# A float32 FNet/SwiGLU mix on one core: the first transform block takes a product of raw data ahead of one of sums, and second forms are made as one row of three results

## The chip, the core and the metric

The kernel runs on one core of one Trainium2 chip. The metric is the device time of one execution in microseconds (us); the median of three runs of the kernel before is 682.49 us.

## The reference, cut to what matters

```
g = sigmoid((x * gate_w).sum(-1))            # x: 2048 x 512, all float32
a = x @ dft_hid_re.T ; b = x @ dft_hid_im.T
y = dft_seq_re @ a - dft_seq_im @ b          # A: the Fourier mixing
h = silu(x @ w1) * (x @ w3)                  # B: w1, w3: 512 x 1376
z = h @ w2                                   # w2: 1376 x 512
out = g * y + (1 - g) * z
```

## The kernel before, in words

**Precision.** TensorE multiplies float32 data rounded to a shorter form (fp32r). Each operand is therefore kept as two parts: the *high* part is the rounded value, made by ScalarE (`high`, L110), and the *low* part is the operand minus its high part, made by VectorE (`low`, L113). `mm3` (L126) makes one product from three matmuls, high x high, high x low and low x high, all issued at L124. In the profile, `zo<-B` on ACT is a high part and `zo<-B,zo` on DVE is a low part.

**Fewer products.** Each matrix product is made in 2 x 2 blocks by the Strassen-Winograd scheme, with seven block products in place of eight. So each operand has forms: four raw blocks (`B11`, `B12`, `B21`, `B22`) and four sums of them (`T1` to `T4`) on the moving side, and seven such forms on the stationary side. VectorE makes the sums (L669 for T1, T2 and T4, L672 for T3).

**Stages.** (1) The gate stage, to about 207 us, makes h for 22 items (11 chunks of w1 and w3, two halves of x). `gate_up(n)` works through item n. Into its lists `early`, `mid` and `at_end` the program puts spare work, such as the forms of w2: for item n of `W2_AT`, `sums_w2` runs in `early` of n, `high_w2` in `mid` of n and `low_w2` in `early` of n+1. (2) The transform stage: blocks 0 to 3 (kind F) multiply the sequence matrices by x, blocks 4 and 5 (H) multiply h by w2, blocks 6 and 7 (Y) apply the hidden matrices.

**The order inside a transform block.** `CHAIN` (L614) lists the seven products with the form of the moving operand that each takes: P1 B11, P5 T1, P6 T2, P3 B22, P7 T3, P2 B21, P4 T4. An F block has 4 steps for each, 28 in all, numbered m; one step is 12 matmuls. Step m needs a tile `zo` with the high and low part of its operand. `advance(m)`, called after the matmuls of step m are issued, loads raw data up to eight steps ahead, makes the sum for step m+4 and splits the operand for step m+3. There are four `zo` tiles, so the high part for step m+4 can be written only when TensorE has finished step m. All engines run their instructions in the order in which the program issues them (`manual_schedule`, L398).

**Stationary forms of x.** Block products P1, P5, P6 and P3 take the forms A1 (made in the gate stage); P7, P2 and P4 take the forms A2, which block 0 itself makes, for eight row groups p = 0 to 7, out of reloaded x (`xs`). `third_a2(p)` makes a 256-wide difference on VectorE (`sum2`, L174), then its high and its low part; `first_a2(p)` splits two raw 256-wide blocks as one 512-wide row. `A2_AT` gives the steps at which load, third and first are issued.

**Results.** When the last step of a product is done, its PSUM banks are read out: P5, P6 and P7 by ScalarE (`read`, L922), and P2, P3, P7 and P4 are finished on VectorE by adds and products with the gate (L929, L954, `spill` L815) and stored. P1, P6, P7 and P4 accumulate in the same pair of banks, P5 and P3 in a second pair, P2 in a third. In block 0, P3's result is put off to step 24 (L947); the other results follow their product at once.

**The start.** Before the loop over items, forms of x (`xo`) are made by hand-placed instructions (L477 to L504); the low part of T1 is put into `early` of item 1 (L510).

Of the kernel before, what the change touches and what calls it, by code (L numbers as in the profile page):

```python
# [21 lines left out]
NG = NST // 2  # L22
# [4 lines left out]
K = 9  # L27
W2_AT = (9, 11, 13, 15)
A1_AT = (12, 14, 16, 17, 18, 19, 20)
A2_AT = ((4, 8, 8), (5, 9, 9), (6, 10, 10), (7, 11, 11),  # L30
         (8, 13, 17), (9, 14, 18), (10, 15, 18), (11, 16, 19))


@with_exitstack
def fnet_swiglu_gate_kernel(
# [20 lines left out]
    nc = tc.nc  # L56
# [52 lines left out]
    def high(hi, src):  # L109
        nc.scalar.activation(hi, src, AF.Copy)  # L110

    def low(hi, lo, src):
        nc.vector.tensor_sub(lo, src, hi.bitcast(F32))  # L113

    def split(hi, lo, src):
        high(hi, src)
        low(hi, lo, src)
# [25 lines left out]
    def flat(ap):  # L143
        return ap.rearrange("p a n -> p (a n)")
# [28 lines left out]

    def sum2(r):  # L174

        nc.vector.tensor_sub(r[:, :256], r[:, 256:512], r[:, :256])  # L176
# [28 lines left out]
    def sum_xo(g, k, t):  # L205
        ST[g, k] = t
        nc.vector.tensor_sub(t, *(ST[g, v] for v in SUMS[k]))  # L207
# [80 lines left out]
    def first2(n):  # L288
        prod(G[n][1], n, 1, 1, False, True)
# [36 lines left out]
    early, ahead, second, mid, at_end = {}, {}, {}, {}, {}  # L326
# [167 lines left out]
    x3 = prod1(3)  # L494
    gate1(1)
    sum_xo(0, "T3", ST[0, "B12"])
    first2(2)
    seed(3, x3)
    high(*xo_parts(0, "T3")[::2])
# [6 lines left out]
    def do(work, n, f, *a):  # L506
        work.setdefault(n, []).append(lambda: f(*a))


    do(early, 1, lambda: low(*xo_parts(0, "T1")))  # L510
    do(ahead, 1, lambda: split_xo(0, "T4"))
    do(second, 1, free, *(ST[0, b] for b in ("B11", "B21", "B12", "B22")))
    do(early, 1, gate1, 2)
# [20 lines left out]
    def w2_parts(p):  # L534
        r, m, t1, t2 = W2R[p]
        return [*((flat(t1[:, 0, i:j]), flat(t1[:, 1, i:j]), v) for i, j, v in
                  ((0, 1, r[:, 256:512]), (1, 4, m[:, :768]))),
                *((flat(t2[:, 0, i:j]), flat(t2[:, 1, i:j]), v) for i, j, v in
                  ((0, 2, r[:, 512:]), (2, 3, r[:, :256])))]

    def sums_w2(p):
        W2R[p] += [wide(f"w2m{p}"), parts(f"w2a{p}"), parts(f"w2b{p}")]
        r, m, t1, t2 = W2R[p]
        sums1(r, m)
        nc.vector.tensor_sub(r[:, :256], r[:, 256:512], r[:, :256])

    def high_w2(p):
        for v in w2_parts(p):
            high(*v[::2])

    def low_w2(p):
        a, b, c, d = w2_parts(p)
        low(*a)
        low(*b)
        nc.gpsimd.dma_start(w2sp[0][p], W2R[p][2].bitcast(F32))
        low(*c)
        low(*d)
        nc.gpsimd.dma_start(w2sp[1][p], W2R[p][3][:, :, :3].bitcast(F32))
        free(*W2R.pop(p))

# [55 lines left out]

    NB = NTB + 4
    KIND = "F" * NTB + "HHYY"
    ORDER = [CHAIN] * (NB - 1) + [tuple(CHAIN[i] for i in (0, 5, 1, 2, 3, 4, 6))]
    NQ = [{"F": NG // 2, "H": NP2 // 2, "Y": KD // 2}[k] for k in KIND]  # L620
    STEPS = [(blk, q, k, form) for blk, nq in enumerate(NQ) for k, form in ORDER[blk]
             for q in range(nq)]
    START = [sum(NQ[:blk]) * len(CHAIN) for blk in range(NB + 1)]

    NEED = [(("B11", 0, 0), ("B12", 1, 1), ("B22", 2, 1), ("B21", 5, 0))] * (NB - 1)
# [4 lines left out]
    LEAD = 3  # L630
    AHEAD = 5
    RESULT = {"P3": 2, "P7": 3, "P2": 0, "P4": 1}
    FORM = {"P1": 0, "P5": 1, "P6": 2, "P3": 3, "P2": 0, "P4": 1, "P7": 2}
    FORMS = {"F": FORM | {"P1": 1, "P5": 3, "P6": 0, "P3": 2}, "H": FORM, "Y": FORM}
    RAW, ZT = {}, {}
    LOADS = sorted((START[blk] + n * nq - e * (blk > 0 or n != 1) + q, blk, k, q)
# [88 lines left out]
            XR[p] = wide(f"xs{p}")  # L725
        nc.sync.dma_start(XR[p], xn[p])

    def third_a2(p):
        A2.append(a2.tile([P, 2, 3, 256], F32R, tag=f"a2_{p}", name=f"a2_{p}"))
        r, t = XR[p], A2[p]  # L730
        sum2(r)
        split(t[:, 0, 2], t[:, 1, 2], r[:, :256])

    def first_a2(p):
        r, t = XR.pop(p), A2[p]
        split(flat(t[:, 0, 0:2]), flat(t[:, 1, 0:2]), r[:, 512:])
        if p >= NG - 1:
            free(r)

# [39 lines left out]

    def late_sums(i):  # L780
        sums1(*LATE[i])
        r = LATE[i][0]
        nc.vector.tensor_sub(r[:, :256], r[:, 256:512], r[:, :256])

    def late_split1(i):

        LATE[i].append(late_pair(i, 0))
        r, m, v = LATE[i]
        splits(*v, r[:, 256:512], m[:, :768])

    def late_split2(i):

        r = LATE[i][0]
        LATE[i].append(late_pair(i, 1))
        splits(*LATE[i][3], r[:, 512:], r[:, :256])

    def late_store(i, j, dst):
        for k, v in enumerate(LATE[i][2 + j]):
# [74 lines left out]
    def step(m):  # L873
        blk, q, k, form = STEPS[m]
        kind = KIND[blk]
        if q == 0 and k == "P6" and kind != "Y":
            load_gate(blk)
        seeded = blk < NB - 1
        if q == 0 and k in ("P1", "P5") + ("P2",) * (not seeded):
            new_banks(k, blk)  # L880
        ps = U[{"P6": "P1", "P7": "P1", "P4": "P1", "P3": "P5"}.get(k, k)]
        zt = ZT.pop(m)
        z = zt.rearrange("p h a n -> p h (a n)")
        own = k in ("P1", "P5") or k == "P2" and not seeded
# [12 lines left out]
        def banks_of(r):  # L897

            if r == 0 or not final:
                return [(ps[r], slice(None), own)]  # L900
            return [(FINAL[1][:, :256], slice(0, 128), True), (ps[1][:, 256:], slice(128, 256), False)]

        for r in range(2):
            sl = slice(r * P, (r + 1) * P)
            for dst, some, new in banks_of(r) if steps else ():
                for n, zn in steps:
                    for i in range(ni):
                        w = ws[2 * n + i]
# [12 lines left out]

        def read(name):  # L922
            res(name)
            for r in range(2):
                nc.scalar.activation(U[name][:, r], ps[r], AF.Copy)  # L925

        def plus(name):
            for r in range(2):
                nc.vector.tensor_add(U[name][:, r], U[name][:, r], ps[r])  # L929

        if k == "P1" and seeded:

            new_banks("P2", blk)
            for r in range(2):
                nc.scalar.activation(U["P2"][r], ps[r], AF.Copy)
        elif k == "P1":
            read("s1")
        elif k == "P5":
            read("p5")
        elif k == "P6":  # L940
            read("u2")
        elif k == "P3":
            def result():
                plus("u2")
                spill(blk, 2, U["u2"])

            result() if blk else todo.setdefault(m + 9, []).append((result, ()))  # L947
        elif k == "P7":
            read("u3")
            if blk == NB - 1:  # L950
                nb = other[blk, RESULT["P4"]][0].rearrange("p (r n) -> p r n", r=2)
                nc.vector.tensor_add(ps[1][:, 256:], ps[1][:, 256:], nb[:, 1, 256:])
                nc.vector.tensor_add(nb[:, 1, :256], nb[:, 1, :256], U["u3"][:, 1, :256])
            nc.vector.tensor_add(flat(U["p5"]), flat(U["p5"]), flat(U["u3"]))  # L954
            spill(blk, 3, U["p5"])
        elif k == "P2" and seeded:
            spill(blk, 0, res("s1"), ps)
        elif k == "P2":
            plus("s1")
            spill(blk, 0, U["s1"])  # L960
        else:
            spill(blk, 1, res("c21"), ps)
# [109 lines left out]
```

## Time and profile before

| quantity | value |
|---|---|
| median of 3 runs | 682.49 us (682.16 to 682.56) |
| the profiled execution: device time | 682.46 us |
| the profiled execution: span in the trace | 680.7 us |
| granted TensorE clock, mean of the core | 1.0 |
| DVE busy, whole span | 582.1 us (86%) |
| ACT busy, whole span | 369.1 us (54%) |
| transform stage, first matmul of block 0 | 207.75 us |

In a row of the timeline the columns are start, length (both in us), engine, line, operation, output<-inputs, shape, and in brackets the idle time of that engine ahead of the row with what ended it. PE is TensorE, PEld its weight loads, DVE VectorE, ACT ScalarE, SPq the DMA issues of SyncE. Matmuls overlap: one of 512 columns is shown as 0.38 us long and the next starts about 0.22 us after it. An idle time on PE is counted from the shown end of the matmul ahead, so the time that is lost is longer than the idle time shown.

### The profile page before, as it was taken

The page shows a single profiled execution, that of the slowest core. Times are in us where ns is not written, and L with a number is a line of the kernel's source. Part 1 is how long each engine was busy: PE and PEld are TensorE (multiplying, and loading weights), DVE is VectorE, ACT ScalarE, POOL GpSimd, SP SyncE. Part 2 cuts the span into 40 slices and gives each one's busy share as a digit, 9 for nine tenths or more (in the row PEclk, how much of TensorE's full clock was granted, in tenths as well). Part 3 has the DMA queues.
Part 4 walks back from the last instruction along what each step waited for, and adds up shares of the span by engine and source line. Part 5 has one row for each costly group of instructions (what it writes and reads, how often), then busy time and mean ns, then how long its engine had stood idle before and what let it go on. Part 6 is the DMA issues. An engine that isn't in the chain of part 4 may idle for free.

```text
span 680.7 us, 8593 instructions
## 1 busy us (share of the span) xinstructions
PE 672.0 (99%) x3101; PEld 582.6 (86%) x3101; DVE 582.1 (86%) x700; ACT 369.1 (54%) x484; POOL 64.1 (9%) x118
## 2 busy tenths in 40 slices
PE   9999999999999999999999999999999999999997
PEld 6888888888888877888888888888888888888886
DVE  6889877777679889997999799978796896898895
ACT  6665565655548555466554654644445455455452
POOL 0021112221010000001020011100000010000000
PEclk9999999999999999999999999999999999999999
DMA  7585566599998644744698169918996871874932
GB/s 293 201 311 221 223 230 226 191 349 381 421 416 288 252 157 156 277 169 158 250 343 331 63 215 340 385 50 337 392 345 237 295 266 75 309 278 156 339 124 92
DMA packets 45562, 172.54 MB, mean 253 GB/s; under 512 B 5328, under 2 KB 5712, under 8 KB 41680
## 3 DMA queue, kind: packets, MB, share of 16 engines
q1 hardware_dynamic: 32480, 118.37, 48.0%
q0 software_dynamic: 12608, 52.97, 19.8%
q10 hardware_dynamic: 432, 0.66, 0.3%
q8 instruction: 24, 0.39, 0.2%
q14 instruction: 18, 0.15, 0.1%
HBM read 114.82 MB, written 57.16 MB: 253 GB/s over the span
## 4 chain that ended last, share of the span: by engine, by line
PE 84%; DVE 10%; issue 2%; DMA 2%; ACT 2%; SPq 0%; ACTq 0%; DVEq 0%
PE P L124 58%; PE X L124 15%; PE Z L124 8%; DVE zo L113 4%; PE Y L124 3%; DVE B L669 2%; DMA xs_B<-xt 1%; DMA B<-cc 1%; ACT zo L110 1%; DVE B L672 1%; DVE a L113 1%; DVE wa L113 1%; DVE xs_B L207 1%; ACT a L110 0%; DVE xs L176 0%
## 5 line engine op out<-in xcount | busy, mean ns | idle before, releaser
L124 PE MATMUL P<-zo,a 128*128 128x512 f32 x1344 | 292.0, 380 | 3.2 <-DVE zo L113 3.1
L124 PEld LDWEIGHTS P<-zo,a 128*128 128x128 f32 x1344 | 253.4, 189 | 41.8 <-DVE zo L113 6.0
L110 ACT ACTIVATE zo<-B 128x1024 fp32r<-128x1024 f32 (+1 forms) x182 | 188.4, 1039 | 170.3 <-PE P L124 83.2
L113 DVE TENSOR_TENSOR zo<-B,zo 128x1024 fp32r<-128x1024 f32 (+1 forms) x182 | 217.5, 1201 | 37.3 <-ACT zo L110 36.9
L124 PE MATMUL P<-zo,H 128*128 128x512 f32 x468 | 101.2, 379 | 0.0
L124 PEld LDWEIGHTS P<-zo,H 128*128 128x128 f32 x468 | 88.5, 189 | 12.6
L669 DVE TENSOR_TENSOR B<-B,B 128x1024 f32<-128x1024 f32 (+1 forms) x78 | 92.7, 1189 | 0.1
L124 PE MATMUL X<-xo,wb 128*128 128x512 f32 x378 | 89.0, 380 | 0.3 <-DVE xo L113 0.3
L124 PEld LDWEIGHTS X<-xo,wb 128*128 128x128 f32 x378 | 71.3, 189 | 11.1 <-DVE xo L113 0.7
L124 PE MATMUL P<-zo,Y 128*128 128x512 f32 (+1 forms) x336 | 71.6, 375 | 0.0
L124 PEld LDWEIGHTS P<-zo,Y 128*128 128x128 f32 x336 | 62.7, 189 | 8.7
L321 POOL DMA_DIRECT2D hsp<-h x42 | 23.1, 549 | 120.8 <-DVE h L378 75.1
L672 DVE TENSOR_TENSOR B<-B,B 128x1024 f32<-128x1024 f32 x26 | 31.7, 1218 | 0.0
L124 PE MATMUL Z<-xo,wb 128*128 128x512 f32 x126 | 30.6, 379 | 0.0
L124 PE MATMUL Z<-xo,wa 128*128 128x512 f32 x126 | 30.6, 379 | 0.0
L124 PE MATMUL Y<-xo,wa 128*128 128x512 f32 x126 | 30.6, 380 | 0.0
L124 PE MATMUL X<-xo,wa 128*128 128x512 f32 x126 | 30.5, 379 | 0.0
L389 ACT ACTIVATE h<-X 128x512 f32<-128x512 f32 x20 | 11.9, 597 | 30.5 <-PE X L124 30.2
L925 ACT ACTIVATE zu<-P 128x512 f32<-128x512 f32 x32 | 18.8, 593 | 15.7 <-PE P L124 15.7
L124 PEld LDWEIGHTS Y<-xo,wa 128*128 128x128 f32 x126 | 23.7, 189 | 3.6 <-ACT Y L285 0.2
L124 PEld LDWEIGHTS X<-xo,wa 128*128 128x128 f32 x126 | 23.8, 189 | 3.4
L124 PEld LDWEIGHTS Z<-xo,wa 128*128 128x128 f32 x126 | 23.8, 189 | 3.4
(149 smaller groups left out, 534.5 us busy)
## 6 DMA issues: line engine op xcount, KB each, us to landing
B<-cc SPq DMA_DIRECT2D x64, 512.0 KB, 6.6
hsp<-h POOLq DMA_DIRECT2D x42, 256.0 KB, 4.2
B<-hsp SPq DMA_DIRECT2D x20, 512.0 KB, 6.8
wbsp<-wb POOLq DMA_DIRECT2D x8, 1024.0 KB, 4.3
wb<-wbsp SPq DMA_DIRECT2D x8, 1024.0 KB, 8.2
B<-zsp SPq DMA_DIRECT2D x16, 512.0 KB, 8.4
H<-w2sp SPq DMA_DIRECT2D x6, 1024.0 KB, 11.0
ws<-w SPq DMA_DIRECT2D x11, 512.0 KB, 5.4
```

Source lines behind the costliest of these rows:

```text
L110: nc.scalar.activation(hi, src, AF.Copy)
L113: nc.vector.tensor_sub(lo, src, hi.bitcast(F32))
L124: nc.tensor.matmul(ps.rearrange("p (n a) -> p n a", a=2), u, turns(v)[:, some], **kw)
L207: nc.vector.tensor_sub(t, *(ST[g, v] for v in SUMS[k]))
L321: nc.gpsimd.dma_start(hsp[g, b + k, j // 2, :, j % 2 * 512 : (j % 2 + 1) * 512], h)
L389: nc.scalar.activation(g1, x, AF.Silu)
L669: nc.vector.tensor_add(t, t, RAW[blk, b, q][:, :n])
L672: nc.vector.tensor_sub(t, RAW[blk, "B12", q], t)
L925: nc.scalar.activation(U[name][:, r], ps[r], AF.Copy)
```

## The change

**Block 0.** Its order of products becomes P1, P5, P6, P3, P2 (B21, raw), P7 (T3), P4 (T4). So eight steps in a row, 12 to 19, take raw operands that need no sum. The loads of B21 move up by four steps. The forms of A2 take the same 512 raw columns and the 256-wide difference as before, but `sum2` now writes the difference next to the raw columns, so that one 768-wide high part and one 768-wide low part make all three. The difference of group p is issued at step 7+p, the high part at 8+p and the low part at 9+p. P3's, P2's and P7's results are put off to steps 24, 25 and 26.

**Elsewhere.** The forms of w2 (gate stage) and of the last w2 and hidden matrices (blocks 1 to 3) are made with the same 768-wide row. For w2 the difference moves out of `sums_w2` into `low_w2`, and its 768-wide high part with it. T1's low part at the start is issued after the sum of T3 and ahead of T3's split.

Cut to its core:

```diff
-A2_AT = ((4, 8, 8), (5, 9, 9), (6, 10, 10), (7, 11, 11),
-         (8, 13, 17), (9, 14, 18), (10, 15, 18), (11, 16, 19))
...
     def sum2(r):
-        nc.vector.tensor_sub(r[:, :256], r[:, 256:512], r[:, :256])
+        nc.vector.tensor_sub(r[:, 256:512], r[:, 256:512], r[:, :256])
...
     sum_xo(0, "T3", ST[0, "B12"])
+    low(*xo_parts(0, "T1"))
...
-    do(early, 1, lambda: low(*xo_parts(0, "T1")))
...
     def sums_w2(p):
...
         sums1(r, m)
-        nc.vector.tensor_sub(r[:, :256], r[:, 256:512], r[:, :256])
...
     def high_w2(p):
-        for v in w2_parts(p):
+        for v in w2_parts(p)[:2]:
             high(*v[::2])
     def low_w2(p):
-        a, b, c, d = w2_parts(p)
+        a, b, c = w2_parts(p)
         low(*a)
+        sum2(W2R[p][0])
+        high(*c[::2])
         low(*b)
...
         low(*c)
-        low(*d)
...
-    ORDER = [CHAIN] * (NB - 1) + [tuple(CHAIN[i] for i in (0, 5, 1, 2, 3, 4, 6))]
+    ORDER = ([tuple(CHAIN[i] for i in (0, 1, 2, 3, 5, 4, 6))] + [CHAIN] * (NB - 2)
+             + [tuple(CHAIN[i] for i in (0, 5, 1, 2, 3, 4, 6))])
...
+        def put(i, f):
+            if blk:
+                f()
+            else:
+                at(0, 24 + i, f)
...
-            result() if blk else todo.setdefault(m + 9, []).append((result, ()))
+            put(0, result)
         elif k == "P7":
...
+            put(2, result)
         elif k == "P2" and seeded:
-            spill(blk, 0, res("s1"), ps)
+            put(1, lambda: spill(blk, 0, res("s1"), ps))
...
-    for p, (load, third, rest) in enumerate(A2_AT):
-        at(0, load, load_a2, p)
-        at(0, third, third_a2, p)
-        at(0, rest, first_a2, p)
+    for p in range(NG):
+        at(0, 4 + p, load_a2, p)
+        at(0, 9 + p, low_a2, p)
+    for p in range(NG):
+        at(0, 8 + p, high_a2, p)
+        at(0, 7 + p, lambda p=p: sum2(XR[p]))
```

The order of VectorE's instructions around steps 8 and 9 of block 0, before (`xs` is reloaded x, `a2` a form of it, `zo11` the operand of step 11, `B22` a raw block):

```order
L113 TENSOR_TENSOR zo10_2061<-B12_0_2_1895,zo10_2061 128x1024
L176 TENSOR_TENSOR xs0_1986<-xs0_1986 128x256
L113 TENSOR_TENSOR a2_0_2067<-xs0_1986,a2_0_2067 128x256
L113 TENSOR_TENSOR a2_0_2067<-xs0_1986,a2_0_2067 128x512
L113 TENSOR_TENSOR zo11_2089<-B12_0_3_1897,zo11_2089 128x1024
L176 TENSOR_TENSOR xs1_2007<-xs1_2007 128x256
L113 TENSOR_TENSOR a2_1_2092<-xs1_2007,a2_1_2092 128x256
L113 TENSOR_TENSOR a2_1_2092<-xs1_2007,a2_1_2092 128x512
L113 TENSOR_TENSOR zo12_2112<-B22_0_0_1899,zo12_2112 128x1024
```

The same place in the changed kernel:

```order
L111 TENSOR_TENSOR zo10_2054<-B12_0_2_1887,zo10_2054 128x1024
L174 TENSOR_TENSOR xs1_1999<-xs1_1999 128x256
L111 TENSOR_TENSOR zo11_2081<-B12_0_3_1889,zo11_2081 128x1024
L111 TENSOR_TENSOR a2_0_2062<-xs0_1978,a2_0_2062 128x768
L174 TENSOR_TENSOR xs2_2020<-xs2_2020 128x256
L111 TENSOR_TENSOR zo12_2102<-B22_0_0_1891,zo12_2102 128x1024
L111 TENSOR_TENSOR a2_1_2087<-xs1_1999,a2_1_2087 128x768
```

A difference stood directly ahead of the two low parts that depend on it; now a split and another form's low part stand between, and there is one low part a group.

VectorE at the end of block 0, before, from the split for step 26 (`zs1` is P2's result, `zu2` P3's):

```order
L113 TENSOR_TENSOR zo26_2398<-B12_0_2_1895,zo26_2398 128x1024
L815 TENSOR_TENSOR zs1_0_2401<-P2_0_0_1982,gate0_0_2075 128x512
L815 TENSOR_TENSOR zs1_0_2401<-P2_0_1_1983,gate0_0_2075 128x512
L929 TENSOR_TENSOR zu2_0_2161<-zu2_0_2161,P5_0_0_1989 128x512
L929 TENSOR_TENSOR zu2_0_2161<-zu2_0_2161,P5_0_1_1990 128x512
L815 TENSOR_TENSOR zu2_0_2161<-zu2_0_2161,gate0_0_2075 128x512 x2
L113 TENSOR_TENSOR zo27_2424<-B12_0_3_1897,zo27_2424 128x1024
L113 TENSOR_TENSOR zo28_2441<-B11_1_0_2339,zo28_2441 128x1024
L113 TENSOR_TENSOR zo29_2458<-B11_1_1_2357,zo29_2458 128x1024
```

And in the changed kernel (`zp5` is P7's result):

```order
L111 TENSOR_TENSOR zo26_2367<-B12_0_2_1887,zo26_2367 128x1024
L925 TENSOR_TENSOR zu2_0_2149<-zu2_0_2149,P5_0_0_1981 128x512
L925 TENSOR_TENSOR zu2_0_2149<-zu2_0_2149,P5_0_1_1982 128x512
L811 TENSOR_TENSOR zu2_0_2149<-zu2_0_2149,gate0_0_2065 128x512 x2
L111 TENSOR_TENSOR zo27_2392<-B12_0_3_1889,zo27_2392 128x1024
L811 TENSOR_TENSOR zs1_0_2395<-P2_0_0_1974,gate0_0_2065 128x512
L811 TENSOR_TENSOR zs1_0_2395<-P2_0_1_1975,gate0_0_2065 128x512
L111 TENSOR_TENSOR zo28_2413<-B11_1_0_2308,zo28_2413 128x1024
L958 TENSOR_TENSOR zp5_0_2057<-zp5_0_2057,zu3_0_2370 128x1024
L811 TENSOR_TENSOR zp5_0_2057<-zp5_0_2057,gate0_0_2065 128x512 x2
L111 TENSOR_TENSOR zo29_2434<-B11_1_1_2326,zo29_2434 128x1024
```

Two results stood between the splits for steps 26 and 27; now one result stands ahead of each of the splits for steps 27, 28 and 29.

VectorE in the gate stage at the start of item 12, before (`w2a` and `w2b` are forms of w2, `xr` reloaded x, `wu` sums for the next weights):

```order
L393 TENSOR_TENSOR h11_1073<-h11_1073,u4_11_1074 128x512
L113 TENSOR_TENSOR w2a1_1085<-w2r1_1070,w2a1_1085 128x256
L113 TENSOR_TENSOR w2a1_1085<-w2m1_1084,w2a1_1085 128x768
L113 TENSOR_TENSOR w2b1_1086<-w2r1_1070,w2b1_1086 128x512
L113 TENSOR_TENSOR w2b1_1086<-w2r1_1070,w2b1_1086 128x256
L170 TENSOR_TENSOR xr0_1149<-xr0_1149 128x256
```

And in the changed kernel:

```order
L389 TENSOR_TENSOR h11_1071<-h11_1071,u4_11_1072 128x512
L111 TENSOR_TENSOR w2a1_1083<-w2r1_1068,w2a1_1083 128x256
L174 TENSOR_TENSOR w2r1_1068<-w2r1_1068 128x256
L111 TENSOR_TENSOR w2a1_1083<-w2m1_1082,w2a1_1083 128x768
L111 TENSOR_TENSOR w2b1_1084<-w2r1_1068,w2b1_1084 128x768
L168 TENSOR_TENSOR xr0_1144<-xr0_1144 128x256
```

The difference (L174) has come into this list out of item 11, and the last low part, now of 768, follows a high part that ScalarE can make only after that difference.

More of the change, by code (lines that the diff above doesn't have):

```diff
@@ L537, in w2_parts @@
                   ((0, 1, r[:, 256:512]), (1, 4, m[:, :768]))),
-                *((flat(t2[:, 0, i:j]), flat(t2[:, 1, i:j]), v) for i, j, v in
-                  ((0, 2, r[:, 512:]), (2, 3, r[:, :256])))]
+                (flat(t2[:, 0, :3]), flat(t2[:, 1, :3]), r[:, 256:])]
     def sums_w2(p):
@@ L623, in fnet_swiglu_gate_kernel @@
     START = [sum(NQ[:blk]) * len(CHAIN) for blk in range(NB + 1)]
-    NEED = [(("B11", 0, 0), ("B12", 1, 1), ("B22", 2, 1), ("B21", 5, 0))] * (NB - 1)
+    NEED = [(("B11", 0, 0), ("B12", 1, 1), ("B22", 2, 1), ("B21", 5 - (b == 0), 0))
+            for b in range(NB - 1)]
     NEED.append((("B11", 0, 0), ("B21", 1, 0), ("B12", 2, 1), ("B22", 3, 1)))
@@ L632, in fnet_swiglu_gate_kernel @@
     RESULT = {"P3": 2, "P7": 3, "P2": 0, "P4": 1}
-    FORM = {"P1": 0, "P5": 1, "P6": 2, "P3": 3, "P2": 0, "P4": 1, "P7": 2}
+    FORM = {"P1": 0, "P5": 1, "P6": 2, "P3": 3, "P7": 0, "P2": 1, "P4": 2}
     FORMS = {"F": FORM | {"P1": 1, "P5": 3, "P6": 0, "P3": 2}, "H": FORM, "Y": FORM}
@@ L726, in load_a2, with a2_parts, high_a2, low_a2 @@
         nc.sync.dma_start(XR[p], xn[p])
-    def third_a2(p):
+    def a2_parts(p):
+        return flat(A2[p][:, 0]), flat(A2[p][:, 1]), XR[p][:, 256:]
+    def high_a2(p):
         A2.append(a2.tile([P, 2, 3, 256], F32R, tag=f"a2_{p}", name=f"a2_{p}"))
[L730 to L736, printed above, removed]
+        high(*a2_parts(p)[::2])
+    def low_a2(p):
+        low(*a2_parts(p))
+        r = XR.pop(p)
         if p >= NG - 1:
@@ L781, in late_sums @@
         sums1(*LATE[i])
-        r = LATE[i][0]
-        nc.vector.tensor_sub(r[:, :256], r[:, 256:512], r[:, :256])
     def late_split1(i):
@@ L789, in late_split1 @@
         splits(*v, r[:, 256:512], m[:, :768])
+        sum2(r)
     def late_split2(i):
-        r = LATE[i][0]
         LATE[i].append(late_pair(i, 1))
-        splits(*LATE[i][3], r[:, 512:], r[:, :256])
+        split(*(t[:, :768] for t in LATE[i][3]), LATE[i][0][:, 256:])
     def late_store(i, j, dst):
@@ L953, in step, with result @@
                 nc.vector.tensor_add(nb[:, 1, :256], nb[:, 1, :256], U["u3"][:, 1, :256])
-            nc.vector.tensor_add(flat(U["p5"]), flat(U["p5"]), flat(U["u3"]))
-            spill(blk, 3, U["p5"])
+            def result():
+                nc.vector.tensor_add(flat(U["p5"]), flat(U["p5"]), flat(U["u3"]))
+                spill(blk, 3, U["p5"])
+            put(2, result)
         elif k == "P2" and seeded:
-            spill(blk, 0, res("s1"), ps)
+            put(1, lambda: spill(blk, 0, res("s1"), ps))
         elif k == "P2":
```

## The prediction

> **What bounds the kernel now.** I read the busy shares first, then who TensorE waits for, then the timeline around those waits.
>
> ```profile
> PE 672.0 (99%) x3101; PEld 582.6 (86%) x3101; DVE 582.1 (86%) x700; ACT 369.1 (54%) x484; POOL 64.1 (9%) x118
> PE P L124 <- DVE zo L113: 3.1, 5, 0.9
> L124 PE MATMUL P<-zo,a 128*128 128x512 f32 x1344 | 292.0, 380 | 3.2 <-DVE zo L113 3.1
> ```
>
> TensorE is the bound almost everywhere, and the change removes no matmul. All it can win is time in which TensorE stands still. The list of waits (second row) has one large entry: five waits in the products with x, for the low part of the moving operand. Their place and true price are in TensorE's timeline:
>
> ```profile
> 207.75 36.65 PE L124 MATMUL P<-zo,a 128*128 128x512 f32 x169
> ...
> 282.84 17.53 PE L124 MATMUL P<-zo,a 128*128 128x512 f32 x80 [0.92 <-DVE zo L113]
> ```
>
> All five lie in block 0: the first row runs for 169 matmuls, that is 14 steps of 12 and one, so the first wait is in step 14, and the last is the one shown. One matmul costs (36.65 - 0.38) / 168 = 0.2159 us, a step of 12 costs 2.591. The matmul that starts at 282.84 is the second of step 27, number 325 after the start of the block (27 x 12 + 1). Without a wait it would start at 207.75 + 325 x 0.2159 = 277.92. So block 0 loses **4.92 us**, more than the 3.1 of shown idle time, because idle is counted from a matmul's shown end and because a short wait can hide between overlapping matmuls.
>
> Why the low parts are late, in VectorE's timeline and in its waits from 205 to 283 us:
>
> ```profile
> 229.63 1.22 DVE L113 TENSOR_TENSOR zo<-B,zo 128x1024 fp32r<-128x1024 f32 x1
> 230.77 0.42 DVE L176 TENSOR_TENSOR xs<-xs 128x256 f32<-128x256 f32 x1
> 231.67 1.22 DVE L113 TENSOR_TENSOR a<-xs,a 128x256 fp32r<-128x256 f32 x2 [0.48 <-ACT a L110]
> 233.13 1.23 DVE L113 TENSOR_TENSOR zo<-B,zo 128x1024 fp32r<-128x1024 f32 x1 [0.25 <-ACT zo L110]
> 234.28 0.42 DVE L176 TENSOR_TENSOR xs<-xs 128x256 f32<-128x256 f32 x1
> DVE a L113 <- ACT a L110: 3.9, 8, 0.5
> DVE zo L113 <- ACT zo L110: 1.5, 5, 0.5
> ```
>
> The split for step 10 ends at 230.85; TensorE needs it with its second matmul, at 207.75 + 121 x 0.2159 = 233.87, so VectorE is 3.0 us ahead. Then each step takes it 234.28 - 230.77 = 3.51 us against TensorE's 2.59, and the lead is gone four steps later. Of the 3.51, 0.73 is standing still: the difference is followed at once by low parts whose high part ScalarE cannot begin before it. Over the block this is 5.4 us (3.9 + 1.5).
>
> **Block 0, part by part.** The prices, start to start: a split or sum of 1024 takes 1.14 (229.63 to 230.77). The other widths are in the gate stage, at the start of item 12:
>
> ```profile
> 126.04 0.42 DVE L113 TENSOR_TENSOR w2a<-w2r,w2a 128x256 fp32r<-128x256 f32 x1
> 126.38 0.95 DVE L113 TENSOR_TENSOR w2a<-w2m,w2a 128x768 fp32r<-128x768 f32 x1
> 127.25 1.02 DVE L113 TENSOR_TENSOR w2b<-w2r,w2b 128x512 fp32r<-128x512 f32 x2
> 128.19 0.42 DVE L170 TENSOR_TENSOR xr<-xr 128x256 f32<-128x256 f32 x1
> ```
>
> So 256 takes 0.34, 768 takes 0.87, and the pair 512 + 256 takes 0.94: the merged low part itself saves only 0.07, eight times, 0.6 us of VectorE. The order is worth far more. A result on VectorE, two instructions of 512, takes 1.20:
>
> ```profile
> 277.97 1.28 DVE L815 TENSOR_TENSOR zs<-P,gate 128x512 f32<-128x512 f32 x2
> 279.17 1.27 DVE L929 TENSOR_TENSOR zu<-zu,P 128x512 f32<-128x512 f32 x2
> 280.37 1.28 DVE L815 TENSOR_TENSOR zu<-zu,gate 128x512 f32<-128x512 f32 x2
> 281.57 4.62 DVE L113 TENSOR_TENSOR zo<-B,zo 128x1024 fp32r<-128x1024 f32 x4
> ```
>
> Before, these three pairs stood ahead of the split for step 27 and made the last wait (split 281.57 to 282.79, matmul 282.84).
>
> Now I run VectorE's lead over TensorE through the new order. Up to the split for step 10 nothing changes but one difference put ahead of it: 3.0 - 0.34 = 2.7. Step 11 has a difference and a split, 1.48 against TensorE's 2.59: 3.8. Steps 12 to 17 have a low part of 768, a difference and a split each, 0.87 + 0.34 + 1.14 = 2.35: a gain of 0.24 a step. No wait is left in them, since a form's difference now stands a step ahead of its high part. Step 18 has no difference (2.01), step 19 the last form, a sum and a split (3.15). Steps 20 to 26 have a sum and a split, 2.28: a gain of 0.31 a step. The sums of T3, which stood among the forms, thus come when the forms are done.
>
> ScalarE sets two limits, from these rows:
>
> ```profile
> L110 ACT ACTIVATE zo<-B 128x1024 fp32r<-128x1024 f32 (+1 forms) x182 | 188.4, 1039 | 170.3 <-PE P L124 83.2
> L110 ACT ACTIVATE w2a<-w2m 128x768 fp32r<-128x768 f32 x4 | 3.4, 840 | 0.9 <-DVE w2m L154 0.9
> 294.58 0.58 ACT L935 ACTIVATE P<-P 128x512 f32<-128x512 f32 x1 [0.19 <-PE P L124]
> 295.88 0.58 ACT L935 ACTIVATE P<-P 128x512 f32<-128x512 f32 x1 [0.71 <-PE P L124]
> ```
>
> With four `zo` tiles, a high part waits for the end of the step four back, so the lead is at most 3 x 2.59 + 0.22, less 0.2 of release, 1.04 of high part and 1.22 of low part: 5.5 us. And for step 15 ScalarE first reads P6 (two of 0.58, after step 11 ends at 238.84), then makes a form's high part (0.84) and the split's (1.04): the low part is ready near 243.4, 3.4 ahead of 246.83. From there the lead goes 3.7, 3.9 and 4.5 (steps 16 to 18), 3.9 (step 19) and up to its limit of 5.5 by step 26. The results cost 2.4, 1.2 and 2.34 ahead of the splits for steps 27, 28 and 29, so it goes 4.6, 4.8, 3.9. No point comes near zero. All five waits go: **-4.9 us** (bounds: 0, if none goes, to -4.9; TensorE cannot run faster than its matmuls).
>
> **The start.** T1's low part moves from 27.61 into the hole ahead of T3's:
>
> ```profile
> 28.24 0.38 PE L124 MATMUL X<-xo,wb 128*128 128x512 f32 x1
> 28.88 1.35 PE L124 MATMUL X<-xo,wb 128*128 128x512 f32 x5 [0.27 <-DVE xo L113]
> 27.73 1.06 ACT L110 ACTIVATE xo<-xs_B 128x1024 fp32r<-128x1024 f32 x1 [0.71 <-DVE xs_B L207]
> 27.61 1.22 DVE L113 TENSOR_TENSOR xo<-t,xo 128x1024 fp32r<-128x1024 f32 x1
> 28.82 1.22 DVE L113 TENSOR_TENSOR xo<-xs_B,xo 128x1024 fp32r<-128x1024 f32 x1
> ```
>
> The wait at 28.88 (0.42 late: due at 28.46) goes, but the next operand is T4. Its high part ends at 28.79 as before, its low part at 30.04; TensorE now needs it at 28.24 + 7 x 0.216 = 29.75 and waits 0.3. Gain **0.1** (0 to 0.4).
>
> **The gate stage.** The new low part of w2 waits for a 768-wide high part, 0.84 long. The rows of item 12, and of the next w2:
>
> ```profile
> 126.53 0.59 ACT L359 ACTIVATE h<-X 128x512 f32<-128x512 f32 x1
> 130.90 0.68 DVE L372 TENSOR_TENSOR u<-u,X 128x512 f32<-128x512 f32 x1
> 132.37 2.10 PE L124 MATMUL X<-xo,wb 128*128 128x512 f32 x9
> 131.48 1.18 SPq L532 DMA_DIRECT2D w2r<-w  x1
> 139.27 0.43 DVE L152 TENSOR_TENSOR w2m<-w2r 128x256 f32<-128x256 f32 x1 [2.01 <-DMA w2r<-w]
> 140.87 0.68 DVE L372 TENSOR_TENSOR u<-u,X 128x512 f32<-128x512 f32 x1
> 140.14 1.46 PE L124 MATMUL Y<-xo,wa 128*128 128x512 f32 x6
> 141.60 2.86 PE L124 MATMUL X<-xo,wb 128*128 128x512 f32 x12
> ```
>
> In item 12: the difference is done at 126.80 (126.38 + 0.42), ScalarE's read of X lets the next start near 127.03 (0.1 ahead of its shown end), the high part is done at 127.87, so the last low part holds VectorE from 127.91 to 128.78, where its predecessor was over at 128.19: VectorE is 0.59 later. Its add to `u` then ends at 132.17 instead of 131.58, and TensorE, which overwrites that bank at 132.37, just does not wait. But the load of the next w2 is queued on SyncE behind a load that waits for VectorE's sums, and goes out 0.59 later. VectorE stands for it at 139.27 already, and through the next add TensorE starts at 141.60 where 141.44 was due. After the change the load lands 0.59 later and the list after it is 0.34 shorter: **+0.25** (from -0.3, if the load lands no later, to +1.0, if items 10 and 16 wait too).
>
> One rule of the Trainium skill ("Perfetto Trace Analysis", Optimizing Scalar/DVE Operations) speaks against the merging here: grouped operations help a saturated engine, but where ScalarE or VectorE aren't saturated and yet hold others up, breaking instructions up lets work be done sooner. By it each of the four merged rows in the gate stage would cost; by the rows above one does.
>
> **Sum.** -4.9 - 0.1 + 0.25 = -4.75 from the profiled 682.46 (span 680.7 and 1.8 around it; the median of the runs is 682.49, the same): **677.7 us**.
>
> **Rivals.**
>
> *A bank read takes the place of the wait.* P7 is now followed by P4, which accumulates in the bank that ScalarE must still read. The rows at 294.58 and 295.88 show such reads half a step apart, each right after its bank is done; the first would be over near 269.4, and TensorE needs that bank at 269.9. If ScalarE is later, behind the split for step 26, both reads are exposed, 1.2 us: 678.9.
>
> *The gate stage pays at all four places*, every delay of VectorE there reaching TensorE. 4 x 0.59 = 2.4, and the start gains nothing: 682.46 - 4.9 + 2.4 = 680.0. Against it: the add to `u` has slack, as computed. This is what the Trainium skill's rule above would give.
>
> *VectorE stays the bound in block 0*, because the waits only move from the forms to the splits, and steps 11 to 18 still take 3.5: 8 x 0.92 less the lead of 2.7 gives 4.7 lost, as before, and the time is 682.4, no change; at half of that excess, 8 x 0.46 less 2.7 gives 1.0 lost, 678.7. For it: ScalarE is in order too. Against it: its load there, a high part of 0.84 and one of 1.04 a step, is under 2.59.
>
> *Gain in the gate stage too*: 0.3 there and 0.4 at the start, 676.9.
>
> *Slower: a reload of x that lands late.*
>
> ```profile
> B<-cc SPq DMA_DIRECT2D x64, 512.0 KB, 6.6
> xs<-xn SPq DMA_DIRECT2D x8, 512.0 KB, 11.6
> ```
>
> The last reload (xs7) now takes the tile of a raw block split for step 13, so it goes out near 237.4, behind a load of B21 that waits for step 12's split; VectorE needs it at 246.5 for the difference, ahead of the split for step 17, with nothing able to pass. Landing times up to 9 us cost nothing, up to 13 only the lead of 3.9; beyond that TensorE waits. From 13 + 4.75 + 1.4 = 19 us on the kernel is slower than before; at 20, 682.46 - 4.75 + 7.0 = 684.7. Against it: both medians above are far below, and 11.6 is that of reloads issued back to back.
>
> TensorE's granted clock stayed 1.0 through waits of 0.9. The Trainium skill ("TensorE: Matmul & The Clock Gate", HAM oscillation) says that a pause over about 3.4 us halves the clock, so such a stall would cost more than its length; no run here shows one.
>
> **How the numbers follow.** The forecast (676.9 to 678.6) gets 0.62, the bank read 0.10, the gate stage 0.10, VectorE as the bound 0.09 (0.05 of it still faster, 0.04 no change), the larger gain 0.05, slower 0.04. A measurement of this kernel can tell 0.2%, 1.4 us, from no change. Faster by more than that: 0.62 + 0.10 + 0.10 + 0.05 + 0.05 = 0.92; same 0.04; slower 0.04. The range, 676.8 to 680.0, holds the forecast, the bank read, the gate stage and the larger gain.
>
> **What would show it.** Right: no wait of TensorE on `zo` between 207 and 283; block 1's matmuls begin about 5 us sooner against the block's start; VectorE without idle time ahead of the low parts of `a`; a wait of about 0.3 left near 29.8; the w2 load of item 13 still waited for. Wrong: a wait of TensorE on ScalarE at the start of step 24; a wait of VectorE on `xs`; any wait left between steps 14 and 27, which would mean that the lead was counted wrongly.

## The result, and the profile after

The changed kernel takes 677.24 us (median of four runs, 677.16 to 677.50), the kernel before 682.44 in runs on the same chip: a ratio of 0.9925, with a 95% interval of 0.9908 to 0.9942. The forecast was 677.7 us in a range of 676.8 to 680.0. The profiled execution has a span of 675.5 us where it was 680.7, at nearly the same granted clock (0.999 where it was 1.000).

The busy shares of the changed kernel, from its page:

```profile
PE 670.4 (99%) x3101; PEld 582.9 (86%) x3101; DVE 580.3 (86%) x682; ACT 367.9 (54%) x466; POOL 64.0 (9%) x118
```

VectorE has 18 instructions fewer but only 1.8 us less to do. The gain of 5.2 us isn't there; it is in who waits for whom. The complete list of TensorE's waits (us in total, times, longest):

```profile
PE wps L400 <- PEq L1069: 0.8, 1, 0.8
PE Z L122 <- DVE xo L111: 0.2, 1, 0.2
```

The row of 3.1 us on `zo` is gone, and block 0 has become one run of matmuls in TensorE's timeline, where six pieces stood with five waits between them:

```profile
207.61 92.77 PE L122 MATMUL P<-zo,a 128*128 128x512 f32 x429
```

The view ends at 300 us, inside block 1. The run starts 0.14 us earlier than before. Without a wait, the second matmul of step 27 comes out at 207.61 + 325 x 0.2159 = 277.78, where 282.84 stood. So 4.92 us are won within block 0, which was all that was lost there. (Of the 0.14, 0.24 was there already at 18.83, where 19.07 stood, ahead of the first instruction that the change moves.)

VectorE's timeline shows where the standing still went, at steps 11 to 15 of block 0:

```profile
231.29 1.22 DVE L111 TENSOR_TENSOR zo<-B,zo 128x1024 fp32r<-128x1024 f32 x1
232.43 0.95 DVE L111 TENSOR_TENSOR a<-xs,a 128x768 fp32r<-128x768 f32 x1
233.30 0.41 DVE L174 TENSOR_TENSOR xs<-xs 128x256 f32<-128x256 f32 x1
233.63 1.22 DVE L111 TENSOR_TENSOR zo<-B,zo 128x1024 fp32r<-128x1024 f32 x1
...
241.21 1.23 DVE L111 TENSOR_TENSOR zo<-B,zo 128x1024 fp32r<-128x1024 f32 x1 [0.47 <-ACT zo L108]
```

A step takes VectorE 233.63 - 231.29 = 2.34 us (3.51 before), with no idle time ahead of a low part of `a`. The last row is the one dip that the prediction foresaw, at step 15. The step in which the lead is smallest, with P7's result ahead of step 29's split:

```profile
275.54 1.22 DVE L958 TENSOR_TENSOR zp<-zp,zu 128x1024 f32<-128x1024 f32 x1
...
278.00 2.35 DVE L111 TENSOR_TENSOR zo<-B,zo 128x1024 fp32r<-128x1024 f32 x2
```

Step 29's low part ends at 278.00 + 1.22 = 279.22. TensorE needs it with matmul 349 of the block, at 207.61 + 349 x 0.2159 = 282.96. The lead is 3.74 us.

The start, in TensorE's timeline:

```profile
29.30 0.38 PE L122 MATMUL Z<-xo,wa 128*128 128x512 f32 x1
29.87 1.35 PE L122 MATMUL Z<-xo,wa 128*128 128x512 f32 x5 [0.20 <-DVE xo L111]
```

As forecast, T1's wait has gone and T4's has come: due at 29.30 + 0.22 = 29.52, it starts 0.35 late, where T1's came 0.42 late.

The gate stage, VectorE's rows in items 12 and 16:

```profile
126.19 0.42 DVE L174 TENSOR_TENSOR w2r<-w2r 128x256 f32<-128x256 f32 x1
...
127.58 0.96 DVE L111 TENSOR_TENSOR w2b<-w2r,w2b 128x768 fp32r<-128x768 f32 x1
128.46 0.42 DVE L168 TENSOR_TENSOR xr<-xr 128x256 f32<-128x256 f32 x1
...
139.12 0.42 DVE L150 TENSOR_TENSOR w2m<-w2r 128x256 f32<-128x256 f32 x1 [1.58 <-DMA w2r<-w]
...
157.15 0.43 DVE L150 TENSOR_TENSOR w2m<-w2r 128x256 f32<-128x256 f32 x1 [2.90 <-DMA w2r<-w]
```

and TensorE's at the same two places:

```profile
141.13 2.85 PE L122 MATMUL X<-xo,wb 128*128 128x512 f32 x12
...
159.35 3.09 PE L122 MATMUL X<-xo,wb 128*128 128x512 f32 x12
```

VectorE's list in item 12 is later, as forecast (128.46 where 128.19 stood, although TensorE runs 0.30 ahead of before here). But the wait near 141 has not grown. It has shrunk: a run of 12 matmuls without a wait is shown as 2.75 us long, so 0.10 is lost in the one at 141.13. A new one stands at 159.35, where 0.34 is lost, since the next w2 was only there at 157.15.

### The profile page after: what moved, and what is told of

Its sections match the earlier page's. It is cut to its first block, busy times and chain, and to the rows that moved or that the text cites. A ratio compares the mean times of both kernels' runs of the same rounds, so it can differ in the third digit from the quotient of the medians.

```text
span 675.5 us, 8569 instructions
## 1 busy us (share of the span) xinstructions
PE 670.4 (99%) x3101; PEld 582.9 (86%) x3101; DVE 580.3 (86%) x682; ACT 367.9 (54%) x466; POOL 64.0 (9%) x118
## 4 chain that ended last, share of the span: by engine, by line
PE 94%; DMA 2%; DVE 2%; issue 0%; ACT 0%; SPq 0%; DVEq 0%
PE P L122 68%; PE X L122 14%; PE Z L122 7%; PE Y L122 3%; DMA wb<-wbsp 1%; DMA xs_B<-xt 1%; DVE xo L111 1%; DVE wa L111 1%; DVE xs_B L203 1%; ACT xo L108 0%; PE P4left L122 0%; SPq L196 0%; DVE t L203 0%; DVE wb L111 0%; SPq L220 0%
```

## The experiments

The theory (A) was that block 0 lost its time because each difference was followed at once by low parts whose high part ScalarE could only make after it; a difference issued a step ahead frees VectorE of that wait. The rivals: the new order of products (B), the merged wider instructions (C), the results put off (D).

**The order of products as before.**

```diff
-    ORDER = ([tuple(CHAIN[i] for i in (0, 1, 2, 3, 5, 4, 6))] + [CHAIN] * (NB - 2)
+    ORDER = [CHAIN] * (NB - 1) + [...]
-    NEED = [(..., ("B21", 5 - (b == 0), 0))
+    NEED = [(..., ("B21", 5, 0))
```

> The changed kernel with only block 0's order of products (and its loads) as before: P7 (T3) again ahead of P2 (B21). Theory A (what freed TensorE is that a form's difference stands a step ahead of its parts, so VectorE no longer waits for ScalarE's answer; the order of products only gives more lead): the four T3 sums cost 1.14 each in steps 12 to 15, the lead falls from 4.6 at the split for step 14 to about 1.3 at the split for step 18 and never reaches zero: 677.2 us, no wait of TensorE in block 0. Theory B (the order is what frees it): 4.6 us of T3 sums are back among the forms and the waits come back: 680 to 682.

Measured: 677.46 us (676.99 to 678.41), ratio 0.993 (0.9916 to 0.9945). TensorE's timeline has no wait in block 0:

```profile
207.27 72.91 PE L122 MATMUL P<-zo,a 128*128 128x512 f32 x337
```

So B is not needed while the differences stand a step ahead.

**The forms as before**, split in two and behind the difference, in the new order of products:

```diff
-    def high_a2(p):
+    def third_a2(p):
...
+        sum2(r)
+        split(t[:, 0, 0], t[:, 1, 0], r[:, 256:512])
...
-        at(0, 9 + p, low_a2, p)
-    for p in range(NG):
-        at(0, 8 + p, high_a2, p)
-        at(0, 7 + p, lambda p=p: sum2(XR[p]))
+        at(0, 8 + p, third_a2, p)
+        at(0, 8 + p, first_a2, p)
```

> The changed kernel with the forms A2 made as before (difference of 256, its high and low part at once, then the 512 raw columns), one group in each of steps 8 to 15, the new order kept. Theory A: VectorE again takes 3.51 us a step for eight steps against 2.59, the lead of 3.0 is gone by the split for step 14, and about 4.4 to 4.9 us are lost: 681.6 to 682.1. Theory B (the order): no wait, 677.2. Theory D (putting off the results): 677.2 as well.

Measured: 683.03 us (682.50 to 685.59), ratio 1.0013 (1.0004 to 1.0023). The gain is gone, and about 1 us more than I expected. TensorE's waits and VectorE's:

```profile
PE P L122 <- DVE zo L111: 3.3, 5, 0.7
PE P L122 <- ACT zu L923: 0.8, 1, 0.8
DVE a L111 <- ACT a L108: 4.1, 8, 0.5
```

The third row is the wait of the theory, once for each of the eight groups. The second row is new: P4, at step 24, waits for ScalarE's read of P7's bank. This is the rival that I had given 0.10, and it stands in a kernel whose lead has gone. The profiled execution is the slowest of the ten, 685.59 us; it came to block 0 2.5 us late (210.14 against 207.61), after a wait of 2.11 us at the very start. In block 0 it loses 5.65 us (matmul 288 starts at 277.97, where 210.14 + 288 x 0.2159 = 272.32 was due), which fits the median: 683.03 - 677.24 = 5.79.

**The forms merged, but behind the difference.**

```diff
-        at(0, 9 + p, low_a2, p)
-    for p in range(NG):
+        at(0, 8 + p, lambda p=p: sum2(XR[p]))
         at(0, 8 + p, high_a2, p)
-        at(0, 7 + p, lambda p=p: sum2(XR[p]))
+        at(0, 8 + p, low_a2, p)
```

> The changed kernel with the merged 768-wide rows, but the difference, the high and the low part of a group issued in one step (steps 8 to 15), so that VectorE must wait for ScalarE's answer to the difference it has just made. Theory A: about 0.45 for the difference, 0.88 of waiting, 0.87 and 1.14, with a little more for the split's own high part, 3.4 a step; eight steps cost 0.83 each less the lead of 3.0: 3.6 to 4.0 us lost, 680.8 to 681.2. Theory C (fewer, wider instructions are what helps): 677.2 to 677.8.

Measured: 682.43 us (682.13 to 682.95), ratio 1.0001 (0.9991 to 1.0010): the whole gain is gone. C falls, as merged instructions alone win nothing. VectorE's wait, and the end of TensorE's timeline in block 0:

```profile
DVE a L111 <- ACT a L108: 7.5, 8, 1.0
```

```profile
258.45 15.59 PE L122 MATMUL P<-zo,a 128*128 128x512 f32 x71 [0.62 <-DVE zo L111]
274.87 1.35 PE L122 MATMUL P<-zo,a 128*128 128x512 f32 x5 [0.82 <-ACT zu L921]
```

A wider high part makes the wait longer, 0.94 us a time instead of the 0.51 of the run before. By 258.45 (matmul 217; the block began at 207.74) 3.86 us are lost to `zo`. The last wait adds 1.09: 258.45 + 71 x 0.2159 = 273.78 was due. ScalarE's timeline shows why it read late:

```profile
273.27 1.06 ACT L108 ACTIVATE zo<-B 128x1024 fp32r<-128x1024 f32 x1 [1.21 <-DVE B L666]
274.23 1.07 ACT L921 ACTIVATE zu<-P 128x512 f32<-128x512 f32 x2
```

The read stands behind the high part of a split, which waits for a sum of the late VectorE. In the changed kernel ScalarE waits for TensorE at this place, not for VectorE.

**Results not put off.** P2's and P7's results go back to where their products end.

```diff
-            if blk:
+            if blk or i:
                 f()
```

> The changed kernel with P2's and P7's results in block 0 made at once, after steps 19 and 23, and not put off to steps 25 and 26 (P3's stays at step 24). Theory A: the lead pays 1.2 after step 19 and, with a wait of 0.9 for ScalarE's read of P7, 5.6 around steps 23 and 24; it starts there at 5.5 and has its own gain on top, about 1.2 is left at the split for step 27: 677.2. Theory D (putting off the results is what takes the last wait away): one wait of about 1 us at step 27 comes back, 678.2 or more.

Measured: 676.73, 676.75 and 676.91 us (a fourth run took 4088 us and is left out), ratio 0.9919 (0.9902 to 0.9935). The extra wait is on VectorE, once, for ScalarE's read of P7, and VectorE has the time:

```profile
DVE zp L958 <- ACT zu L921: 0.9, 1, 0.9
```

TensorE does not wait in block 0.

D falls: with the forms' lead, putting off isn't needed.

**The kernel before, with only its differences a step ahead.**

```diff
         r, t = XR[p], A2[p]
-        sum2(r)
...
         at(0, load, load_a2, p)
+        at(0, third - 1, lambda p=p: sum2(XR[p]))
```

> The kernel before with one line moved: the difference of each reloaded x is taken one step ahead of its forms. Products, widths, results and gate stage stay as before. Theory A (the wait on ScalarE's high part behind the difference is what made VectorE slow): its steps 11 to 14 take 0.34 + 0.94 + 1.14 = 2.42 instead of 3.51, steps 15 to 18 with a sum 2.96, the lead never reaches zero, all of the 4.9 us in block 0 is won: 677.4 to 677.7. Theory B (order of products), C (merged forms) or D (results put off), if one of them were needed as well: 679 to 682.4.

Measured: 677.52 us (677.49 to 678.12), ratio 0.9930 (0.9916 to 0.9943). This one moved line does what the whole change does. TensorE's timeline has no wait in block 0 (the view ends at 340), and VectorE's shows one step:

```profile
207.81 132.48 PE L124 MATMUL P<-zo,a 128*128 128x512 f32 x613
```

```profile
231.16 1.01 DVE L113 TENSOR_TENSOR a<-xs,a 128x256 fp32r<-128x256 f32 x2
232.09 0.41 DVE L176 TENSOR_TENSOR xs<-xs 128x256 f32<-128x256 f32 x1
...
233.57 1.01 DVE L113 TENSOR_TENSOR a<-xs,a 128x256 fp32r<-128x256 f32 x2
```

A step takes 233.57 - 231.16 = 2.41 us, as worked out (2.42), under TensorE's 2.59, with the old widths.

**Differences back and products in the old order.** The edit of the third experiment with that of the first.

> The changed kernel with two parts undone: each difference stands directly ahead of its merged high and low part again, and the products of block 0 go in the old order (B21's raw product behind T3's). With the new order and the differences put back, 3.86 us were lost to the waits on zo and 1.09 to the wait of step 24's P4 on ScalarE's read of P7's bank. Theory E (a late ScalarE makes the wait on P7's bank, and only where P4 follows P7 at once): that wait is gone, the waits on zo stay, 681.1. Rival (the loss is VectorE's total in the block and shows up at whichever wait comes next): 682.2 to 682.4, as with the new order.

Measured: 685.57 us (685.04 to 686.03), ratio 1.0043 (1.0026 to 1.0060). Both numbers were missed. TensorE's waits, and VectorE's timeline at step 16:

```profile
PE P L122 <- DVE zo L111: 6.8, 5, 1.7
```

```profile
249.38 0.42 DVE L174 TENSOR_TENSOR xs<-xs 128x256 f32<-128x256 f32 x1
...
251.63 1.22 DVE L668 TENSOR_TENSOR B<-B,B 128x1024 f32<-128x1024 f32 x1
...
253.90 0.41 DVE L174 TENSOR_TENSOR xs<-xs 128x256 f32<-128x256 f32 x1
```

The wait on P7's bank is gone, as Theory E said, though ScalarE is also no longer late at that point, so order and lateness aren't told apart by it. What I had overlooked is the second row: in the old order T3's sums fall among steps that carry a form, and each of these takes VectorE 253.90 - 249.38 = 4.52 us. At the last wait (263.08, matmul 217, from 208.18) 8.05 us are lost instead of 3.86. So where VectorE has no lead, the new order saves 4.2 us of waits on `zo` but brings the bank wait of 1.09: 3.1 us in all (685.57 - 682.43). Where VectorE has a lead, it is worth nothing.

**w2 in the gate stage as before.**

```diff
-                (flat(t2[:, 0, :3]), flat(t2[:, 1, :3]), r[:, 256:])]
+                *((flat(t2[:, 0, i:j]), flat(t2[:, 1, i:j]), v) for i, j, v in
+                  ((1, 3, r[:, 512:]), (0, 1, r[:, :256])))]
...
         sums1(r, m)
+        nc.vector.tensor_sub(r[:, :256], r[:, 256:512], r[:, :256])
...
-        a, b, c = w2_parts(p)
+        a, b, c, d = w2_parts(p)
         low(*a)
-        sum2(W2R[p][0])
-        high(*c[::2])
...
+        low(*d)
```

> The changed kernel with the gate stage's forms of w2 made as before: three high parts early, the difference among the sums of item 11, and low parts of 512 and 256 apart. My step said that the merged low part delays VectorE by 0.59 us in item 12 and that this costs 0.25 us through the next w2 load. By that step: VectorE's list of item 12 ends 0.57 us sooner than in the changed kernel, the load of the next w2 goes out about 0.5 us sooner, and the time is 0.1 to 0.3 us under the changed kernel: 676.9 to 677.1. By the rule that every merged row in the gate stage costs its delay (4 x 0.59): 674.9. By a third view, that the landing time of the w2 loads, which differed by up to 2 us between kernels with the same gate stage, decides these waits: the same 677.2 within 0.2, with a wait of TensorE near 141 or 159 us present or absent by the landing and not by the merge.

Measured: 677.33 us (677.01 to 677.59), ratio 0.9924 (0.9911 to 0.9938): the third view. VectorE's rows in items 12 and 13, and TensorE's:

```profile
128.06 0.41 DVE L168 TENSOR_TENSOR xr<-xr 128x256 f32<-128x256 f32 x1
...
139.13 0.43 DVE L150 TENSOR_TENSOR w2m<-w2r 128x256 f32<-128x256 f32 x1 [2.00 <-DMA w2r<-w]
```

```profile
141.47 2.86 PE L122 MATMUL X<-xo,wb 128*128 128x512 f32 x12
...
159.70 2.75 PE L122 MATMUL X<-xo,wb 128*128 128x512 f32 x12
```

VectorE is 0.40 us sooner (0.57 against TensorE's matmuls, which run 0.17 later here). The w2 load goes out sooner, too, by SyncE's timeline of this kernel:

```profile
131.35 1.16 SPq L528 DMA_DIRECT2D w2r<-w  x1
```

and of the changed one:

```profile
131.76 1.15 SPq L528 DMA_DIRECT2D w2r<-w  x1
```

But it is in use at 139.13, where it was at 139.12. The stall near 141 is there without the merge, and the one at 159 is not.

The profiles of the other kernels with the merged rows show how much this differs with the same instructions. Between 135 and 165 us TensorE loses nothing in four of them (the old order, the results not put off, and three and five more low parts), and 0.97 us in the one with six more. There the w2 load that goes out at 143.77 is in use only at 157.97; with five more it goes out at 143.59 and is in use at 154.51.

**More work for VectorE at step 29**, where its lead is smallest: the low part issued k = 3, 6 and 5 times more.

```diff
-            low(t[:, 0, :n], t[:, 1, :n], src[:, :n])
+            for _ in range({1+k} if m == 29 else 1):
+                low(t[:, 0, :n], t[:, 1, :n], src[:, :n])
```

Three more:

> The changed kernel with the low part of step 29's split issued three times more (the same values written again): 3 x 1.14 = 3.42 us more of VectorE at the point where its lead over TensorE is smallest, 3.75 us by the trace. If the lead is what the trace says, nothing is lost: 677.2, and no wait of TensorE at step 29. If VectorE's work there were exposed at all (no lead, or a lead under 2 us), 1.5 to 3.4 us are lost: 678.7 to 680.7, with a wait on zo at step 29.

Measured: 677.23 us (677.15 to 677.43), ratio 0.9924 (0.9910 to 0.9937). No wait is shown: TensorE's timeline has one run,

```profile
207.27 122.98 PE L122 MATMUL P<-zo,a 128*128 128x512 f32 x568
```

It is (122.98 - 0.38) - 567 x 0.2159 = 0.18 us longer than its matmuls take, too little to show as idle time. The delay falls at step 29: matmul 348, the last ahead of the one that needs the low part, starts on time, and matmul 352 starts 0.19 late. So three more use the lead up almost exactly.

Six more:

> The same with six more: 6.84 us of VectorE against a lead of 3.75. If the lead is what the trace says: 3.1 us lost and about 0.1 for the restart, 680.3 to 680.5, in one wait of TensorE on zo at step 29. If the lead were longer than the trace says, less; if extra work on VectorE were paid in full: 684.1.

Measured: 683.38 us (681.58 to 684.04), ratio 1.0012 (1.0003 to 1.0021), 6.1 us lost instead of 3.1. VectorE's timeline shows seven writes of step 29 and one of step 30, and in a view from 287.4 on the last two of the eight; TensorE's shows the pause:

```profile
278.81 9.91 DVE L111 TENSOR_TENSOR zo<-B,zo 128x1024 fp32r<-128x1024 f32 x8
286.36 2.36 DVE L111 TENSOR_TENSOR zo<-B,zo 128x1024 fp32r<-128x1024 f32 x2
```

```profile
208.41 75.50 PE L122 MATMUL P<-zo,a 128*128 128x512 f32 x349
287.64 42.53 PE L122 MATMUL P<-zo,a 128*128 128x512 f32 x188 [3.72 <-DVE zo L111]
```

Due at 208.41 + 349 x 0.2159 = 283.76, TensorE starts 3.88 late. The seven writes start (286.36 - 278.81) / 6 = 1.26 us apart, not 1.14: each starts just after the one ahead (1.22 long) has ended. 6 x 1.26 - 3.74 = 3.82, and TensorE starts 0.06 after the last one's end (286.36 + 1.22 = 287.58). So the lead is as the trace said. The next expectation puts a repeat at 1.24 and the restart at 0.17, which adds up to the same within 0.01. But the 188 matmuls behind the pause take (42.53 - 0.38) - 187 x 0.2159 = 1.78 us too long, and a table of windows (start:end, length, then PE, PEld, DVE, ACT and POOL busy with their counts, granted clock, DMA share, GB/s) shows what they met:

```profile
289.00:290.00 1.00, 1.00 (x4) 0.73 (x4) 1.00 (x3) 0.00 (x0) 0.00 (x0) 0.50 0.02 8
...
291.00:292.00 1.00, 1.00 (x4) 0.82 (x3) 1.00 (x2) 0.84 (x1) 0.00 (x0) 0.50 0.60 246
292.00:293.00 1.00, 1.00 (x5) 0.83 (x5) 1.00 (x2) 0.22 (x1) 0.00 (x0) 0.82 0.69 279
```

TensorE's granted clock is halved for some 3.4 us. This run also came to block 0 0.80 us later than the changed kernel, 0.53 of it at the w2 load (0.97 lost there against 0.44); 3.88 + 1.78 + 0.80 = 6.46 of the 6.5 by which its span is longer.

Five more, to tell lead and clock apart:

> The changed kernel with the low part of step 29's split issued five times more. The trace of the run with six showed one repeat to take 1.24 us (it waits for its predecessor's end), a lead of 3.74 us used up, a pause of 3.88 us and then TensorE's granted clock at 0.50 from 289 to 292.3 us, 1.7 us more. If lead and clock are two separate terms: 5 x 1.24 - 3.74 + 0.17 = 2.6 us lost in one pause on zo, a granted clock of 1.0 after it, 679.9. If the extra loss came with the extra work itself and not with the length of the pause: the clock falls here too, about 681.5. If the lead were other than 3.74, the pause differs by that much.

Measured: 681.19 us (679.64 to 681.66 in seven runs), ratio 0.9975 (0.9964 to 0.9986). TensorE's timeline and its windows (PE alone):

```profile
207.21 75.50 PE L122 MATMUL P<-zo,a 128*128 128x512 f32 x349
285.18 15.12 PE L122 MATMUL P<-zo,a 128*128 128x512 f32 x61 [2.46 <-DVE zo L111]
```

```profile
286.00:287.00 1.00, 1.00 (x4) 0.50 1.03 414
...
288.00:289.00 1.00, 1.00 (x4) 0.61 0.08 31
```

The pause costs 285.18 - 282.56 = 2.62 us, exactly as worked out from the lead. I expected a full clock behind it, and that was wrong: it is halved in this execution, too, for (15.12 - 0.38) - 60 x 0.2159 = 1.79 us. But not in each: the two fastest runs, 679.64 and 680.11 us with a mean granted clock of 0.999, are where 677.24 + 2.62 = 679.9 lies, and the slowest, 681.66 with 0.997, where the halved clock's 1.8 comes on top. A clock halved for 3.4 us takes 0.0025 off the mean, so the mean clock tells three such runs (681.23, 681.31 and 681.66, at 0.996 or 0.997) from four without (all at 0.999). One of these four took 681.19, the median; why is not known. So the loss isn't tied to the extra work alone. At this pause it strikes in some executions only.

## Why the prediction was right

**Block 0, -4.9.** Right: all five waits went, 4.92 us. The cause is A: a difference a step ahead is enough, and without it nothing is won. The kernel before with its differences moved wins the same; merged instructions without the move win nothing; the order of products and the results put off can each be undone at no cost.

**VectorE's lead.** The step of 2.35 us was measured as 2.34, the lead ahead of step 29 as 3.74 instead of 3.9, and three, five and six repeats confirm it to 0.2 us. Step 15 was off, 4.25 instead of 3.4: ScalarE began to read P6 half a step sooner than I had put it, since a product's first bank is done half a step ahead of its second. Its timeline:

```profile
237.78 0.58 ACT L921 ACTIVATE zu<-P 128x512 f32<-128x512 f32 x1
238.90 0.60 ACT L921 ACTIVATE zu<-P 128x512 f32<-128x512 f32 x1 [0.54 <-PE P L122]
```

**The start, -0.1.** Right in kind: T4's wait took the place of T1's, 0.07 us are won.

**The gate stage, +0.25.** The step that failed is "the load lands 0.59 later and the list after it is 0.34 shorter". VectorE was later by what was worked out, and the load went out later, but its landing did not follow: issued at 131.76 or 131.35, it was in use at 139.12 or 139.13. (The list after it is shorter, as forecast: 1.26 us from there to the add to `u`, where it was 1.60.) The stalls that the profiled execution shows, 0.10 and 0.34 us where 0.27 stood near 141, come and go with the landing, and with w2 made as before the median is the same within 0.1. The size of the term is 0 within the 0.2 that such medians scatter. That the two profiled executions differ by 0.17 at these stalls (0.44 against 0.27), near the 0.25, says little: with the same merged rows other profiles lose from 0 to 0.97. Without the term the sum is 682.44 - 4.92 - 0.07 = 677.45, and 677.24 was measured.

**The bank read, rival at 0.10.** It did not come, because ScalarE was not late. Its price was right: 1.09 us in the kernel with merged forms behind their differences, against the 1.2 forecast.

**The gate stage at all four places.** It did not come: undoing the merge there would have won 2.4 us and won nothing. The rule named there, of the Trainium skill's "Perfetto Trace Analysis", Optimizing Scalar/DVE Operations, is not borne out here: with the forms behind their differences, the rows broken up were no faster than the merged ones (683.03 us against 682.43). What helped in block 0 was to issue an instruction sooner, not to break one up. Where the differences stood a step ahead, merged and unmerged rows took the same within 0.3 us (677.24 and 677.52), and so they did in the gate stage.

**VectorE stays the bound, and the late reload.** Neither came: a step takes 2.34 us, and VectorE never waits on `xs`.

## What to carry to other kernels

Look for an engine that makes a value, which a second engine then works on, and whose next instruction needs that second engine's answer. Here VectorE stood still 0.51 or 0.94 us each time. Issue the instruction that makes the value one step ahead, with other work between. The whole of a many-part change may hang on that one move, and its other parts may only be worth something without it: undo each alone, and undo them together. To know whether an engine off the path has room, write down its lead at each step; repeats of one of its instructions at the smallest lead test the figure.

## What the runs showed of the hardware

A pause of TensorE of 2.1 us or more can halve its granted clock for some 3.4 us once it works again; the two pauses at step 29 cost 1.8 us each on top. With 3.88 us lost, the mean clock shows it in nine of ten runs (682.68 to 684.04 us, 0.996 or 0.997; the tenth had 1.000 and 681.58), and with 2.62 in three of seven. The profiled execution of the forms made as before has it at its very start, after a wait of 2.11 us and without any extra work of VectorE (the second row is a window for PE alone):

```profile
7.02 2.59 PE L122 MATMUL C<-xo,wa 128*128 128x512 f32 x6 [2.11 <-ACT xo L108]
8.00:9.00 1.00, 1.00 (x4) 0.50 1.04 426
```

It never came with waits of 1.67 us shown (the differences put back in the old order: a granted clock of 1.00 from 240 to 300 us).

The Trainium skill ("TensorE: Matmul & The Clock Gate", HAM oscillation) puts the bound at pauses of about 3.4 us. Here it was crossed sooner; the measurement decides. The same page says (The HAM clock gate) that the window in which activity is counted runs freely, and that the number of slow matmuls at a kernel's start therefore differs between runs of one kernel; that a pause of one length strikes in some runs only would fit that. How much of a window must be idle was not measured.

Waits hide more than they show. With the differences put back and the old order, five waits of 6.8 us shown cost 8.05; in the kernel with merged forms behind their differences, 2.6 shown cost 3.86.

On VectorE, a 1024-wide instruction that writes what the one directly ahead wrote starts 1.26 us after it, instead of 1.14 (the run with six more).
